# Attention and gated feed-forward on one core: the last third of a unit's gate and value pieces moved into the next unit, ahead of its output products

## The chip, the cores and the metric

The kernel runs on one core of one Trainium2 chip. The time is that of the device for one execution, in microseconds (us), the median of several runs. The profile is one execution of the same program; its span is a little under the run's time (377.5 us of span for a run of 379.3). Engines are called as in the profile: PE is TensorE's matmuls, PEld its weight loads, DVE is VectorE, ACT ScalarE, POOL GpSimd, SP the queue that starts transfers. The granted clock is the share of its full clock at which TensorE was let run.

## The reference

```
# q, k, v: 4 batches x 8 heads x 768 tokens x 64; 16 centroids a head
mask   = cluster(q) == cluster(k)             # a query sees the keys of its own cluster
attn   = softmax(where(mask, q k^T / 8, -1e9)) v
x      = attn, heads side by side             # 3072 tokens x 512
xn     = x / sqrt(mean(x*x) + 1e-6) * rms_g
g, val = xn w_gate, xn w_val                  # 512 -> 1536
out    = (g * sigmoid(g) * val) w_out         # 1536 -> 512
```

## The kernel before

The work is cut into eight units, each half of a batch's queries (384) with all eight heads. In unit u the attention of u is issued step by step (8 heads x 3 steps of two scores matmul blocks), and between the steps a list called `fill` is worked off: the feed-forward layer of the units before. The fill of a unit is spread over the 24 steps by weights.

```python
ps_s = pool("ps_s", 2, space=PSUM)      # scores
ps_a = pool("ps_a", 1, space=PSUM)      # probabilities x values
ps_g = pool("ps_g", 3, space=PSUM)      # everything else, three buffers in rotation
...
def rms(u):                              # RMS step of unit u
    x = xs[u]
    for t in range(HT):
        squares(u, t, True)              # ScalarE
    ...                                  # VectorE: sum, mean, rsqrt (3 Newton steps of 3 operations)
    for t in range(HT):
        nc.vector.tensor_scalar_mul(xn[u][:, t], x[:, t], y[:, t:t + 1])
...
def gv(u, f, val):                       # one piece: four matmuls, a PSUM buffer, a VectorE reader
    ...
    ps = ps_g.tile([P, UQ], F32, tag="gen", name="val" if val else "gate")
    for c in range(CC):
        nc.tensor.matmul(ps, lhsT=w[:, c, f * P:(f + 1) * P], rhs=xnT[u][:, c], ...)
    ...
    if not val:                          # (not the last unit)
        ...
        nc.scalar.activation(th, ps, ACT.Tanh, scale=0.5)
        nc.vector.scalar_tensor_tensor(th, th, 1.0, ps, op0=ALU.add, op1=ALU.mult)
        ...
    else:
        nc.vector.scalar_tensor_tensor(gvT[u][:, f], gates[u], 0.5, ps, op0=ALU.mult, op1=ALU.mult)
...
def out_mm(u, t, part):                  # an output product in three parts of four matmuls
    ...                                  # part 0 takes a buffer of ps_g
    for f in range(4 * part, 4 * part + 4):
        nc.tensor.matmul(outs[u], lhsT=gvT[u][:, f, ...], rhs=wo[:, f], ...)
    if part == 2:
        ...
        nc.vector.tensor_copy(o, outs[u])
        ...
        nc.sync.dma_start(out=..., in_=o)
...
for u in range(NU):
    fill = []
    if u >= 2:
        fill += out_work(u - 2)
    ...
        fill += spread(ffn_work(u - 1), prep)
    ...
    for h in range(H):
        for i in range(3):
            scores(u, h, i)
            if i == 1 and (u, h) != (0, 0):
                pv(u, h - 1) if h else pv(u - 1, H - 1)   # ends with inv and x on VectorE
            if (h, i) == (0, 1) and u:
                rms(u - 1)
            ...
            while n < len(fill) and done <= total * (3 * h + i + 1) / gaps:
                done += fill[n][0]
                fill[n][1]()
                n += 1
    ...
pv(NU - 1, H - 1)
rms(NU - 1)
for _, f in out_work(NU - 2) + ffn_work(NU - 1) + out_work(NU - 1):   # the tail
    f()
```

The traces show VectorE keeping the order of this program. In unit 7 of the kernel before, the first output product was complete at about 304.7 us, and its copy started at 309.81, behind xn, which stands ahead of it.

The softmax here doesn't subtract the row's maximum and nothing guards it: scores larger than these inputs give would overflow.

Of the kernel before, what the change touches and what calls it, by code (L numbers as in the profile page):

```python
# [22 lines left out]
def kernel(  # L23
# [23 lines left out]
    NU = 2 * B  # L47
    CC = DM // P
    FC = DF // P
    scale = 1.0 / (D ** 0.5)  # L50
    KR = D + NC
    WARM = 5
    NQ, NV = 6, 8

    ctx.enter_context(tc.manual_schedule())
# [46 lines left out]
    def busy(n, first=True):  # L102
        to = ps_a.tile([P, 512], F32, tag="acc", name="warm") if first else \
            ps_g.tile([P, 512], F32, tag="gen", name="warm")
        for i in range(n):
            nc.tensor.matmul(to, lhsT=warm[:, :P], rhs=warm, start=True, stop=True)

    busy(WARM)

# [142 lines left out]
    def scores(u, h, i):  # L252
        b, hf = divmod(u, 2)
        g, hh = b * 2 + h // HG, h % HG
        if i == 0:
            pT[u, h] = ptp.tile([P, ST, UQ], BF16, tag="pT", name="pT")
        ps = ps_s.tile([P, 2, 512], F32, tag="s", name="s")
        for j in range(2):
            kc = 2 * i + j
            nc.tensor.matmul(ps[:, j, :UQ], lhsT=kext[g % 4][:KR, hh, kc * P:(kc + 1) * P],  # L260
                             rhs=qext[g % 4][:KR, hh, hf * UQ:(hf + 1) * UQ], start=True, stop=True)
        nc.scalar.activation(pT[u, h][:, 2 * i:2 * i + 2], ps[:, :, :UQ], ACT.Exp, bias=off, scale=scale * ZS)  # L262
# [3 lines left out]
    def pv(u, h):  # L266
        b = u // 2
        g, hh = b * 2 + h // HG, h % HG
        if h == 0:
            xs[u] = xp.tile([P, HT, DM], F32, tag="x", name="x", bufs=2)  # L270
        if h % 2 == 0:
            accs[u] = ps_a.tile([P, 2, HT, D + 1], F32, tag="acc", name="acc")
        acc = accs[u]
        for t in range(HT):
            for kc in range(ST):
                nc.tensor.matmul(acc[:, h % 2, t], lhsT=pT[u, h][:, kc, t * P:(t + 1) * P],  # L276
                                 rhs=vbf[g % 4][:, hh, kc % HT * 2 + kc // HT], start=kc == 0, stop=kc == ST - 1)
        if h % 2:
            inv = small.tile([P, 2, HT], F32, tag="inv", name="inv")
            invs[u] = inv  # L280
            nc.vector.reciprocal(inv, acc[:, :, :, D])
            dst = xs[u][:, :, (h - 1) * D:(h + 1) * D].rearrange("p t (h d) -> p h t d", d=D)
            nc.vector.tensor_tensor(dst, acc[:, :, :, :D], inv.unsqueeze(3).broadcast_to([P, 2, HT, D]), op=ALU.mult)  # L283
# [28 lines left out]
    def xtrans(u, c):  # L312
        if c == 0:
            xnT[u] = xp.tile([P, CC, UQ], BF16, tag="xnT", name="xnT")
        ps = ps_g.tile([P, UQ], BF16, tag="gen", name="tx")
        for t in range(HT):
            nc.tensor.transpose(ps[:, t * P:(t + 1) * P], xn[u][:, t, c * P:(c + 1) * P], ident)  # L317
        nc.vector.tensor_scalar_mul(xnT[u][:, c], ps, gcol[:, c:c + 1])
# [3 lines left out]
    def gv(u, f, val):  # L322
        if f == 0 and not val:
            gvT[u] = xp.tile([P, FC, UQ], BF16, tag="gvT", name="gvT")
        w = wv if val else wg
        ps = ps_g.tile([P, UQ], F32, tag="gen", name="val" if val else "gate")
        for c in range(CC):
            nc.tensor.matmul(ps, lhsT=w[:, c, f * P:(f + 1) * P], rhs=xnT[u][:, c], start=c == 0, stop=c == CC - 1)  # L328
        last = u == NU - 1
        if not val:  # L330
            th = ffn.tile([P, UQ], F32, tag="th", name="th")
            if last:
                nc.scalar.activation(th, ps, ACT.Silu)
                gates[u] = th
# [3 lines that stand above are left out]
                gates[u] = th  # L338
        elif last:
            nc.vector.tensor_mul(gvT[u][:, f], gates[u], ps)  # L340
        else:
            nc.vector.scalar_tensor_tensor(gvT[u][:, f], gates[u], 0.5, ps, op0=ALU.mult, op1=ALU.mult)  # L342
# [3 lines left out]
    def out_mm(u, t, part):  # L346
        b, hf = divmod(u, 2)
        if part == 0:
            outs[u] = ps_g.tile([P, DM], F32, tag="gen", name="o")
        for f in range(4 * part, 4 * part + 4):  # L350
            nc.tensor.matmul(outs[u], lhsT=gvT[u][:, f, t * P:(t + 1) * P], rhs=wo[:, f], start=f == 0, stop=f == FC - 1)  # L351
        if part == 2:
            o = outp.tile([P, DM], F32, tag="o_sb", name="o_sb")
            nc.vector.tensor_copy(o, outs[u])  # L354
            rows = out[b * S:(b + 1) * S].rearrange("(p t) f -> p t f", t=ST)
            nc.sync.dma_start(out=rows[:, 2 * t + hf], in_=o)


    def group_work(g):
        w = []  # L360
        for h in range(HG):
            n = g * HG + h
            w.append((0.25, lambda h=h: trans(g, h, 0)))

            def second(h=h, n=n):
                trans(g, h, 1)
                qcast(g, h)
                kcast(g, h)
                vcast(n)
                load_qk(n + NQ)  # L370
                load_v(n + NV)
            w.append((0.25, second))
        w.append((0.7, lambda: scores_c(g, 0)))
        w.append((0.7, lambda: (scores_c(g, 1), place(nc.gpsimd, nc.gpsimd if g > 1 else nc.sync))))
        return w

    def spread(a, b):

        if not a:
            return list(b)  # L380
        w, n = [], 0
        for i, x in enumerate(a):
            w.append(x)
            while n < len(b) * (i + 1) // len(a):
                w.append(b[n])
                n += 1
        return w

    def ffn_work(u):
        w = [(0.18, lambda c=c: xtrans(u, c)) for c in range(CC)]  # L390
        for f in range(FC):
            w.append((0.64, lambda f=f: gv(u, f, False)))
            w.append((0.64, lambda f=f: gv(u, f, True)))
        return w

    def out_work(u):
        return [(0.86, lambda t=t, p=p: out_mm(u, t, p)) for t in range(HT) for p in range(3)]
# [49 lines left out]
    def second_group():  # L447
        kcast(0, 2, True)
        kcast(0, 3, True)
        for m in range(2):  # L450
            scores_c(1, m)
        for c in range(CC):
            load_gv(c)
        for n in range(HG, H):
            vcast(n)
        place(nc.sync, nc.sync)
        for h in range(HG):
            kcast(1, h)
# [14 lines left out]
    for u in range(NU):  # L473
        fill = []
        if u >= 2:
            fill += out_work(u - 2)
        prep = group_work(u + 2) if 2 <= u < NG - 2 else []
        if u == 0:
            for i in range(2 * H - 6):
                fill += [(0.0 if i else 8.0, lambda: None), (1.0, lambda: busy(1, False))]  # L480
        elif u == 1:
            prep = group_work(2) + group_work(3)
            f0 = ffn_work(0)
            fill = [(0.5, f) for _, f in prep[:8]] + f0[:12] + [(0.0, output_weights)] + spread(f0[12:], prep[8:])
        else:
            fill += spread(ffn_work(u - 1), prep)
        total = sum(c for c, _ in fill)
        gaps, done, n = 3 * H, 0.0, 0
        for h in range(H):
            for i in range(3):  # L490
                scores(u, h, i)
                if (u, h, i) == (0, 0, 1):
                    second_group()
                if i == 1 and (u, h) != (0, 0):
                    pv(u, h - 1) if h else pv(u - 1, H - 1)
                    if (u, h) == (0, 6):
                        second_batch()
                if (h, i) == (0, 1) and u:
                    rms(u - 1)
                if h == H - 1:  # L500
                    squares(u, i, False)
# [4 lines that stand above are left out]
        for _, f in fill[n:]:  # L506
            f()
    pv(NU - 1, H - 1)
    rms(NU - 1)
    for _, f in out_work(NU - 2) + ffn_work(NU - 1) + out_work(NU - 1):  # L510
        f()


# [28 lines left out]
```

## Time and profile before

| | before |
|---|---|
| time | 380.02 us (377.32 to 380.52) |
| span of the profiled run | 377.5 us |
| TensorE busy | 94% of the span |
| ScalarE, VectorE busy | 69%, 63% |
| mean granted TensorE clock | 0.973 |

The page's slices (40 equal ones; each digit the busy share in tenths, PEclk the granted clock in tenths) of the kernel before:

```profile
PE   6979758999989999999999999999999999998995
PEclk9985986999999999999999999999999999999999
```

After slice 9 TensorE is nearly full (eight tenths or more in every slice but the last) and its clock too. What TensorE waited for, the two longest sums (line waited for: us in total, times, longest):

```profile
PE s L260 <- ACT pT L262: 3.6, 5, 2.2
PE tx L317 <- DVE xn L308: 3.2, 2, 2.8
```

No single one of these sums comes to 4 us in 377. The cuts into units and their openings are shown in the prediction.

### The profile page before, as it was taken

The page shows a single profiled execution, that of the slowest core. Times are in us where ns is not written, and L with a number is a line of the kernel's source. Part 1 is how long each engine was busy: PE and PEld are TensorE (multiplying, and loading weights), DVE is VectorE, ACT ScalarE, POOL GpSimd, SP SyncE. Part 2 cuts the span into 40 slices and gives each one's busy share as a digit, 9 for nine tenths or more (in the row PEclk, how much of TensorE's full clock was granted, in tenths as well). Part 3 has the DMA queues.
Part 4 walks back from the last instruction along what each step waited for, and adds up shares of the span by engine and source line. Part 5 has one row for each costly group of instructions (what it writes and reads, how often), then busy time and mean ns, then how long its engine had stood idle before and what let it go on. Part 6 is the DMA issues. An engine that isn't in the chain of part 4 may idle for free.

```text
span 377.5 us, 7991 instructions
## 1 busy us (share of the span) xinstructions
PE 353.5 (94%) x3026; PEld 212.9 (56%) x3026; DVE 238.6 (63%) x573; ACT 261.3 (69%) x461; POOL 107.4 (28%) x221
## 2 busy tenths in 40 slices
PE   6979758999989999999999999999999999998995
PEld 2535445566556655665566655665556656664552
DVE  3882057786766777668766777659756655666432
ACT  4697973789667876788667875888757875882330
POOL 2595062086633135322713134221700000000000
PEclk9985986999999999999999999999999999999999
DMA  7549999726133212232031002000020002001002
GB/s 258 171 105 198 237 334 269 151 60 195 34 121 98 89 43 95 70 125 65 21 128 43 2 9 98 2 0 4 21 84 2 3 5 81 2 0 58 28 3 83
DMA packets 24967, 32.03 MB, mean 85 GB/s; under 512 B 4960, under 2 KB 20832, under 8 KB 24928
## 3 DMA queue, kind: packets, MB, share of 16 engines
q1 hardware_dynamic: 18288, 24.72, 20.0%
q0 software_dynamic: 6064, 6.00, 8.5%
q10 hardware_dynamic: 576, 0.79, 0.6%
q8 instruction: 24, 0.39, 0.4%
q14 instruction: 15, 0.12, 0.1%
HBM read 28.35 MB, written 6.29 MB: 92 GB/s over the span
## 4 chain that ended last, share of the span: by engine, by line
PE 75%; DVE 10%; ACT 6%; DMA 5%; issue 2%; SPq 1%; DVEq 0%; ACTq 0%
PE gate L328 17%; PE val L328 16%; PE s L260 14%; PE o L351 10%; PE acc L276 8%; PE tq L195 5%; PE sc L221 4%; ACT pT L262 3%; DMA qk<-in_q_dram 2%; DMA out_dram<-o_sb 2%; DVE o_sb L354 2%; ACT junk L295 2%; DVE xn L308 1%; PE tx L317 1%; DVE x L283 1%
## 5 line engine op out<-in xcount | busy, mean ns | idle before, releaser
L262 ACT ACTIVATE pT<-s,off 128x768 bf16<-128x768 f32 x192 | 170.9, 901 | 45.0 <-PE s L260 44.5
L260 PE MATMUL s<-qext,kext 80*128 80x384 bf16 x384 | 97.3, 337 | 3.9 <-ACT pT L262 3.6
L328 PE MATMUL gate<-xnT,wg 128*128 128x384 bf16 x384 | 79.2, 327 | 2.1 <-ACT qkT L197 2.1
L328 PE MATMUL val<-xnT,wv 128*128 128x384 bf16 x384 | 78.4, 326 | 0.0
L337 DVE SCALAR_TENSOR_TENSOR th<-th,gate 128x384 f32<-128x384 f32 x84 | 46.4, 552 | 49.3 <-ACT th L336 48.5
L351 PE MATMUL o<-wo,gvT 128*128 128x512 bf16 x288 | 69.3, 379 | 0.0
L201 POOL CAST qext<-qkT 64x384 bf16<-64x384 f32 x64 | 33.4, 522 | 99.8 <-ACT qkT L197 97.9
L260 PEld LDWEIGHTS <-kext 80*128 80x128 bf16 x384 | 37.1, 100 | 38.6 <-issue 14.0
L336 ACT ACTIVATE th<-gate 128x384 f32<-128x384 f32 x84 | 40.9, 487 | 20.4 <-PE gate L328 20.2
L342 DVE SCALAR_TENSOR_TENSOR gvT<-th,val 128x384 bf16<-128x384 f32 x84 | 46.4, 552 | 8.2 <-PE val L328 1.6
L276 PEld LDWEIGHTS <-pT 128*128 128x128 bf16 x1152 | 45.8, 100 | 10.2 <-issue 1.7
L328 PEld LDWEIGHTS <-wg 128*128 128x128 bf16 x384 | 36.4, 97 | 25.4 <-issue 4.0
L328 PEld LDWEIGHTS <-wv 128*128 128x128 bf16 x384 | 36.1, 98 | 23.2 <-issue 2.0
L276 PE MATMUL acc<-vbf,pT 128*128 128x65 bf16 x1152 | 47.7, 196 | 0.5 <-ACT pT L262 0.5
L351 PEld LDWEIGHTS <-gvT 128*128 128x128 bf16 x288 | 27.1, 97 | 27.9
L245 POOL DMA_DIRECT2D qext<-oh x56 | 27.5, 496 | 50.1 <-DVE oh L233 50.0
L197 ACT COPY qkT<-tq 128x384 f32<-128x384 f32 x64 | 29.5, 481 | 13.5 <-PE tq L195 13.0
L195 PE MATMUL tq<-ident_f,qk 128*128 128x128 f32 x192 | 33.3, 294 | 4.4 <-DMA qk<-in_q_dram 3.0
L195 PEld LDWEIGHTS tq<-ident_f,qk 128*128 128x128 f32 x192 | 24.0, 149 | 14.5 <-DMA qk<-in_q_dram 2.6
L209 DVE TENSOR_SCALAR kext<-qkT 64x384 bf16<-64x384 f32 x56 | 21.2, 379 | 9.5 <-ACT qkT L197 8.7
L245 POOL DMA_DIRECT2D kext<-oh x48 | 23.3, 491 | 13.1 <-DVE oh L233 11.4
L354 DVE COPY o_sb<-o 128x512 f32<-128x512 f32 x24 | 15.8, 683 | 16.9 <-DMA out_dram<-o_sb 6.4
(60 smaller groups left out, 232.8 us busy)
## 6 DMA issues: line engine op xcount, KB each, us to landing
qk<-in_q_dram SPq DMA_DIRECT2D x32, 192.0 KB, 3.8
vs<-in_v_dram SPq DMA_DIRECT2D x32, 192.0 KB, 3.7
out_dram<-o_sb SPq DMA_DIRECT2D x24, 256.0 KB, 2.0
qk<-in_k_dram SPq DMA_DIRECT2D x28, 192.0 KB, 3.6
wg<-in_moe_w_gate_dram POOLq DMA_DIRECT2D x4, 384.0 KB, 9.1
wv<-in_moe_w_val_dram POOLq DMA_DIRECT2D x4, 384.0 KB, 10.4
wo<-in_moe_w_out_dram POOLq DMA_DIRECT2D x3, 512.0 KB, 13.4
qext<-oh POOLq DMA_DIRECT2D x56, 12.0 KB, 1.7
```

What stands on the lines that cost most here:

```text
L195: nc.tensor.transpose(ps[:, i * P:(i + 1) * P], qk[:, part, 2 * i:2 * i + 2].rearrange("p t d -> p (t d)"), ident_f)
L197: nc.scalar.copy(qkT[g, h // 2][:, h % 2, part], ps)
L201: nc.gpsimd.tensor_copy(qext[g % 4][:D, h, e * UQ:(e + 1) * UQ], qkT[g, h // 2][e * D:(e + 1) * D, h % 2, 0])
L245: on.dma_start(out=ext[D:D + NC, h, e * UQ:(e + 1) * UQ], in_=oh[32 * h + e * NC:32 * h + (e + 1) * NC])
L260: nc.tensor.matmul(ps[:, j, :UQ], lhsT=kext[g % 4][:KR, hh, kc * P:(kc + 1) * P], rhs=qext[g % 4][:KR, hh, hf * UQ:(hf + 1) * UQ], start=T ...
L262: nc.scalar.activation(pT[u, h][:, 2 * i:2 * i + 2], ps[:, :, :UQ], ACT.Exp, bias=off, scale=scale * ZS)
L276: nc.tensor.matmul(acc[:, h % 2, t], lhsT=pT[u, h][:, kc, t * P:(t + 1) * P], rhs=vbf[g % 4][:, hh, kc % HT * 2 + kc // HT], start=kc == 0 ...
L328: nc.tensor.matmul(ps, lhsT=w[:, c, f * P:(f + 1) * P], rhs=xnT[u][:, c], start=c == 0, stop=c == CC - 1)
L336: nc.scalar.activation(th, ps, ACT.Tanh, scale=0.5)
L337: nc.vector.scalar_tensor_tensor(th, th, 1.0, ps, op0=ALU.add, op1=ALU.mult)
L342: nc.vector.scalar_tensor_tensor(gvT[u][:, f], gates[u], 0.5, ps, op0=ALU.mult, op1=ALU.mult)
L351: nc.tensor.matmul(outs[u], lhsT=gvT[u][:, f, t * P:(t + 1) * P], rhs=wo[:, f], start=f == 0, stop=f == FC - 1)
```

## The change

The intent can be guessed from the diff: a part of the feed-forward work that is left over from one unit comes first in the next, so that the fill of unit 1 is lighter and there is TensorE work ahead of the output products.

```diff
+    CUT = CC + 2 * FC - 8
...
         if u >= 2:
-            fill += out_work(u - 2)
+            fill += ffn_work(u - 2)[CUT:] + out_work(u - 2)
...
-            f0 = ffn_work(0)
+            f0 = ffn_work(0)[:CUT]
...
-            fill += spread(ffn_work(u - 1), prep)
+            fill += spread(ffn_work(u - 1)[:CUT], prep)
...
-    for _, f in out_work(NU - 2) + ffn_work(NU - 1) + out_work(NU - 1):
+    for _, f in ffn_work(NU - 2)[CUT:] + out_work(NU - 2) + ffn_work(NU - 1) + out_work(NU - 1):
```

`ffn_work` has 4 transposes and 24 gate and value pieces; `CUT` leaves the last 8 pieces (f = 8 to 11) out. The RMS step keeps its place, in the second step of a unit, and ahead of everything in the tail.

## The prediction

> **What bounds the kernel now.** I cut the run into its units first. The chain of work that ended last shows a block of eight output-product matmuls (line L351) at 94.74, 137.37, 179.49, 221.54, 263.66 and 301.22 us; each opens a unit of the loop, so units 2 to 7 begin just before these times, unit 1 fills 50 to 94.7, and the tail after the loop 338.1 to 377.5. The busy time of each engine in these stretches (columns: stretch, its length, then busy us of PE, PEld, DVE, ACT, POOL, then the granted clock, DMA share, GB/s):
>
> ```profile
> 50.00:94.70 44.70, 39.63 (x366) 25.11 (x364) 32.85 (x76) 32.44 (x59) 20.64 (x40) 0.92 0.73 197
> 137.30:179.40 42.10, 41.39 (x378) 25.58 (x377) 29.46 (x72) 31.58 (x57) 13.74 (x28) 1.00 0.26 81
> ...
> 301.20:338.10 36.90, 36.24 (x335) 22.31 (x333) 21.93 (x55) 27.62 (x49) 0.00 (x0) 1.00 0.06 22
> 338.10:377.50 39.40, 33.50 (x200) 17.72 (x198) 17.18 (x42) 9.67 (x22) 0.00 (x0) 1.00 0.11 41
> ```
>
> TensorE idles about 0.7 us in a unit of 42.1, and the clock is full. Busy matmul time can flatter, so I checked it by pace. One gate or value piece (four matmuls) takes 0.65 us in the chain, an output piece 0.86, a pair of scores matmuls 0.33, a block of 18 probability-value matmuls 0.55 (timeline, start to the next start). For unit 7: 24 x 0.65 + 9 x 0.86 + 24 x 0.33 + 8 x 0.55 = 35.7, plus 12 transposes of about 0.06, is 36.4 of 36.9 us. So in units 2 to 7 TensorE sets the time, without slack: whatever stops it for a microsecond costs a microsecond. Second, I read what the other engines do at the opening of a unit, for there the change works. Unit 7, in order of time:
>
> ```profile
> 301.06 1.89 PE L351 MATMUL o<-wo,gvT 128*128 128x512 bf16 x8
> ...
> 303.12 0.71 PE L276 MATMUL acc<-vbf,pT 128*128 128x65 bf16 x18
> ...
> 304.10 0.56 DVE L283 TENSOR_TENSOR x<-acc,inv 128x384 f32<-128x384 f32 x1
> ...
> 306.05 0.16 DVE L302 TENSOR_TENSOR sm<-ss 128x3 f32<-128x3 f32 x1 [1.40 <-ACT junk L295]
> ...
> 308.62 1.28 DVE L308 TENSOR_SCALAR xn<-x,ny 128x512 bf16<-128x512 f32 x3
> ...
> 309.81 1.28 DVE L354 COPY o_sb<-o 128x512 f32<-128x512 f32 x2
> ```
>
> The last head of the former unit arrives (acc), VectorE scales it (x), waits 1.40 us for ScalarE's squares, runs a chain of small operations, and writes xn: from 304.66 to 309.90, VectorE serves nobody else. The first output product was complete by about 304.7, yet its copy comes after xn at 309.81: VectorE keeps program order. TensorE does not feel it, because three output products of 2.6 us each have three PSUM buffers (ps_g, three slots in rotation) and need no reader until the third is done.
>
> [...]
>
> ```profile
> 57.09 0.29 PE L317 MATMUL tx<-ident,xn 128*128 128x128 bf16 x1 [2.82 <-DVE xn L308]
> ```
>
> (the timeline of TensorE), and in the busy times by microsecond, whose first column after the engines is the clock:
>
> ```profile
> 57.00:58.00 1.00, 0.55 (x2) 0.21 (x2) 1.00 (x4) 0.00 (x0) 1.00 (x2) 0.50 1.06 381
> ...
> 62.00:63.00 1.00, 1.00 (x5) 0.47 (x4) 0.00 (x0) 0.24 (x1) 0.00 (x0) 0.50 1.12 209
> 63.00:64.00 1.00, 1.00 (x6) 0.49 (x4) 0.55 (x1) 0.85 (x2) 0.00 (x0) 0.69 1.14 245
> ```
>
> A wait of 2.82 us for xn in unit 1 is followed by clock 0.50 from about 56.8 to 63.6[...]. A wait of 2.20 us at 22.8 us has 0.50 from 26.1 to 36.3[...]; two of 0.51 and 0.99 us close together before 46.5 have it from 46.6 to 50.0[...]; one of 1.50 us in the tail has none. [...] the trace has just three table loads, and the last (1283 ns, for Silu in the tail) has time to spare, so I count nothing for tables.
>
> **The change, part by part.** No operation is added or removed. Of the 24 gate and value pieces of a unit, 8 (f = 8 to 11) move into the next unit, before its output pieces.
>
> Unit 1 loses 8 x 0.65 = 5.2 us of TensorE work, units 2 to 7 lose 8 and gain 8, the tail gains 8. The fill per step of unit 1 falls from 24.88/24 = 1.04 to 19.76/24 = 0.82 weight units, so its wait for xn shrinks by perhaps 0.9 us (one pair of scores and one block of 18 come ahead of it), but the second half has denser transposes, with short waits for ScalarE's copies. I choose -5.2 for unit 1.
>
> Opening of units 2 to 7. A gate or value piece needs a PSUM buffer like an output product, but a new one every piece, and it is freed by VectorE operations (552 ns each, lines L337 and L342) that stand in VectorE's queue by program order. By the weights 0.64 and the loop's rule, two pieces (gate 8, value 8) are issued before the RMS chain; gate 9 and value 9 directly behind it; then gate 10, value 10. With time 0 at the unit's first scores pair: gate 8 and value 8 end at 1.63, scores at 1.96, the block of 18 at 2.5. ScalarE's queue (the former unit's Exp and a Square, as at 300.5 to 302.7 now) lets Tanh 8 finish at about 2.4, VectorE's two operations on it end at 3.6, and only then x follows: 4.4, against 3.9 now (304.66 less the unit's first scores pair, 300.73). From x to xn's end is 5.24 us as read above: 9.65. The reader of gate 9 is next: 10.2. TensorE meanwhile writes gate 9, value 9 (its buffer was gate 8's) and gate 10 (value 8's), and comes to value 10 at 4.8 to 5.1; its buffer is gate 9's. It stops until 10.2, so for 5.1 to 5.4 us, say 5.2. From the idle 0.6 to 0.7 us of now I take back 0.3, the waits of the transposes at the end of the output products, since the copies now come in time. Net 4.9 x 6 = 29.4 us. After the stop VectorE is one piece ahead again and no second stop follows.
>
> Tail. Now TensorE runs output products for 7.8 us under the chain, then waits 1.50 us:
>
> ```profile
> 347.14 0.50 PE L317 MATMUL tx<-ident,xn 128*128 128x128 bf16 x6
> 348.40 0.69 DVE L354 COPY o_sb<-o 128x512 f32<-128x512 f32 x1 [1.59 <-DMA out_dram<-o_sb]
> 349.14 0.65 PE L317 MATMUL tx<-ident,xn 128*128 128x128 bf16 x6 [1.50 <-DVE o_sb L354]
> ```
>
> After it, all eight pieces come behind the chain: gate 8, value 8 and gate 9 fill the buffers from 339.4 to 341.35, value 9 waits for the reader of gate 8, which follows xn's end at 345.6 and takes 0.55: a stop of 4.85 us. The five pieces left are paced by VectorE at up to 1.1 us a pair and end at about 349.3, so the output products begin 9.9 us later than now; the transposes behind them save about 0.8 of the 1.50. Net 9.1.
>
> Clock. [...] I put the end of the drop 3.3 to 6.7 us after work resumes, mean 5; at half clock this loses 2.5 us, a little less where TensorE has gaps: 2.3 x 7 = 16 us. This is an estimate from the three drops' lengths in this trace.
>
> Sum: 380.0 - 5.2 + 29.4 + 9.1 + 16 = 429; rounded down for stops that run partly under the drop: 427.
>
> **The rivals.** Work is only rearranged: TensorE is full, unit 1 loses 5.2, the tail gains 5.2 less 0.8, and each unit saves its 0.3: about 377, or within 2%. For it speaks that counts and bytes are equal, and that pieces in the tail would cover the RMS chain; against it that these pieces need VectorE, which the output products did not. Second rival: the stop comes but the clock holds: 413. Against it are drops after 2.20 and 2.82 us; for it, none after 1.50. Third: the lost time is ScalarE's, because Exp, Tanh and squares crowd at the opening; but ScalarE is busy 31.6 of 42.1 us and the same pieces leave the unit's end, so it would cost under 1 us a unit: 382.
>
> **Range and chances.** Without drops 413[...]. I take 411 to 438. The order of VectorE's queue and the three buffers are read, not guessed, so slower by over 2% gets 0.92, within 2% 0.05, faster 0.03.
>
> **What would show it.** Right: in each of units 2 to 7 a TensorE wait of about 5 us at a value piece, released by L337 of VectorE, directly behind xn; units of about 47 us, or 49 with clock 0.50 after the stop; a stop near 5 us in the tail; unit 1 some 5 us shorter; output copies no longer held by xn. Wrong: no such wait (more buffers in effect, or another order on VectorE), stops of under 2 us, or clock 1.00 throughout units 2 to 7.

No term of the sum is cut: 380.0 - 5.2 + 29.4 + 9.1 + 16 = 429, rounded down to 427. The 16 us for the clock is the author's estimate. It has a drop at each of the seven stops, since waits of 2.20 and 2.82 us had been followed by one and the stops are longer; the 3.3 to 6.7 us until the clock comes back are estimated from the lengths of that trace's three lows, 10.2, 3.4 and 6.8 us (26.1 to 36.3, 46.6 to 50.0, 56.8 to 63.6), and what sets the end of a low was not shown. The upper end of the range, 438, was the estimate for lows as long as the longest of these at every stop.

## The result, and the profile after

The changed kernel takes 428.5 us (427.37 to 429.53, four runs) against 378.67 of the kernel before (four runs), ratio 1.132 with a 95% interval of 1.124 to 1.139. Ratios here are the mean time of one kernel's fast runs over that of the other's of the same rounds, so not quite the ratio of the medians. It is correct, and slower by about 50 us. Forecast were 427.

The slices of the changed kernel:

```profile
PE   7979669976999499995999779995999689959996
PEclk9968989996999979996999969998899979998999
```

Where the kernel before has an almost unbroken row of nines, there is now a hole every four to five slices (a slice is 10.6 us, a unit 44 to 51), and the clock dips with it. TensorE's longest waits:

```profile
PE val L329 <- DVE th L338: 37.5, 8, 5.4
PE s L261 <- ACT pT L263: 3.9, 6, 2.2
```

The first line is new: value pieces wait for VectorE's operation on the gate (lines have moved by one: L329 is the old L328). The same cut into units (columns as in the prediction: stretch, length, busy us of PE, PEld, DVE, ACT, POOL, clock, DMA share, GB/s), for unit 1, unit 3, unit 7 and the tail:

```profile
44.12:87.56 43.44, 35.87 (x349) 22.39 (x348) 29.12 (x69) 33.50 (x63) 19.65 (x37) 0.96 0.74 195
...
138.07:188.06 49.99, 44.37 (x381) 26.70 (x377) 30.27 (x71) 32.35 (x57) 13.68 (x29) 0.93 0.22 68
...
331.61:376.20 44.59, 38.99 (x341) 23.64 (x339) 23.00 (x56) 28.73 (x49) 0.00 (x0) 0.92 0.05 19
376.20:425.60 49.40, 39.91 (x226) 21.16 (x226) 21.19 (x50) 10.97 (x26) 0.00 (x0) 0.95 0.09 33
```

Unit 3 has the same number of VectorE and ScalarE instructions, within one, as before, but takes 49.99 us instead of 42.1, at a clock of 0.93; TensorE's busy time grew too, from 41.4 to 44.4 us, for the same matmuls. The opening of unit 6 in order of time:

```profile
291.11 0.56 DVE L284 TENSOR_TENSOR x<-acc,inv 128x384 f32<-128x384 f32 x1
...
291.34 0.81 PE L329 MATMUL gate<-xnT,wg 128*128 128x384 bf16 x4
...
293.06 0.16 DVE L303 TENSOR_TENSOR sm<-ss 128x3 f32<-128x3 f32 x1 [1.40 <-ACT junk L296]
...
295.77 1.31 DVE L309 TENSOR_SCALAR xn<-x,ny 128x512 bf16<-128x512 f32 x3
...
297.00 0.53 DVE L338 SCALAR_TENSOR_TENSOR th<-th,gate 128x384 f32<-128x384 f32 x1
297.58 1.44 PE L329 MATMUL val<-xnT,wv 128*128 128x384 bf16 x4 [5.11 <-DVE th L338]
```

The gate piece at 291.34 (gate 10) is the last that finds a PSUM buffer. Its follower, value 10, wants the buffer of gate 9, whose reader is the th at 297.00, directly behind xn. TensorE waits 5.11 us, then needs 1.44 us for four matmuls that took 0.81: the clock stands at 0.50. The clock is the column after the five engines:

```profile
293.00:294.00 1.00, 0.00 (x0) 0.00 (x0) 0.81 (x4) 1.00 (x3) 1.00 (x4) 1.00 0.13 33
294.00:295.00 1.00, 0.00 (x0) 0.00 (x0) 0.82 (x6) 1.00 (x3) 1.00 (x3) 0.76 0.11 25
...
298.00:299.00 1.00, 1.00 (x5) 0.46 (x4) 0.66 (x2) 0.00 (x0) 0.00 (x0) 0.50 0.00 0
...
301.00:302.00 1.00, 1.00 (x20) 0.86 (x19) 0.42 (x1) 0.88 (x1) 0.00 (x0) 0.83 0.00 0
```

It falls to 0.50 within the stop, at 294.5, and returns to 1.00 at 301.35, 3.8 us after the work did. The tail has the same stop, and the old wait at the transposes behind the output products shrinks from 1.50 to 0.45 us:

```profile
381.99 1.28 DVE L309 TENSOR_SCALAR xn<-x,ny 128x512 bf16<-128x512 f32 x3
383.18 0.55 DVE L338 SCALAR_TENSOR_TENSOR th<-th,gate 128x384 f32<-128x384 f32 x1
383.78 1.44 PE L329 MATMUL val<-xnT,wv 128*128 128x384 bf16 x4 [4.63 <-DVE th L338]
...
397.16 0.65 PE L318 MATMUL tx<-ident,xn 128*128 128x128 bf16 x6 [0.45 <-DVE o_sb L355]
```

Where the 48.0 us between the two profiled spans come from, by the starts of the units' first scores matmul (the tail from the start of the last block of 18; by this cut unit 1 of the kernel before begins at 45.06, not at 50):

| part | forecast | measured |
|---|---|---|
| up to unit 1 | 0 | -0.9 |
| unit 1 | -5.2 | -5.7 |
| units 2 to 7 | 29.4 and 13.8 for the clock | 7.9, 7.9, 6.8, 7.9, 7.1, 6.8: together 44.3 |
| tail | 9.1 and 2.3 for the clock | 10.4 |

### The profile page after: what moved, and what is told of

Same layout as the page of the kernel before. It is cut to its first block, busy times and chain, and to the rows that moved or that the text cites. A ratio compares the mean times of both kernels' runs of the same rounds, so it can differ in the third digit from the quotient of the medians.

```text
span 425.6 us, 7990 instructions
## 1 busy us (share of the span) xinstructions
PE 366.6 (86%) x3026; PEld 216.4 (51%) x3026; DVE 243.0 (57%) x573; ACT 264.2 (62%) x461; POOL 107.7 (25%) x221
## 4 chain that ended last, share of the span: by engine, by line
PE 62%; DVE 24%; ACT 9%; issue 3%; DMA 2%; SPq 0%; DVEq 0%; ACTq 0%
PE o L352 15%; PE val L329 12%; PE gate L329 11%; PE s L261 11%; PE acc L277 7%; PE tq L196 4%; ACT pT L263 4%; ACT junk L296 3%; DVE th L338 3%; DVE xn L309 3%; DVE gvT L343 3%; DVE ohT L231 2%; DVE oh L234 2%; DVE mx L229 2%; DVE scT L225 1%
## 5 line engine op out<-in xcount | busy, mean ns | idle before, releaser
L329 PE MATMUL val<-xnT,wv 128*128 128x384 bf16 x384 | 84.9, 347 | 37.8 <-DVE th L338 37.5
L261 PE MATMUL s<-qext,kext 80*128 80x384 bf16 x384 | 99.5, 344 | 4.0 <-ACT pT L263 3.9
L329 PE MATMUL gate<-xnT,wg 128*128 128x384 bf16 x384 | 83.9, 342 | 2.0 <-DVE xnT L319 1.4
L329 PEld LDWEIGHTS <-wv 128*128 128x128 bf16 x384 | 38.6, 102 | 67.6 <-issue 46.9
L343 DVE SCALAR_TENSOR_TENSOR gvT<-th,val 128x384 bf16<-128x384 f32 x84 | 46.5, 554 | 12.9 <-PE val L329 5.9
L277 PEld LDWEIGHTS <-pT 128*128 128x128 bf16 x1152 | 46.6, 101 | 10.6 <-issue 2.4
L329 PEld LDWEIGHTS <-wg 128*128 128x128 bf16 x384 | 37.7, 101 | 25.6 <-issue 7.9
L198 ACT COPY qkT<-tq 128x384 f32<-128x384 f32 x64 | 29.4, 482 | 6.1 <-PE tq L196 5.5
L210 DVE TENSOR_SCALAR kext<-qkT 64x384 bf16<-64x384 f32 x56 | 22.3, 398 | 14.8 <-ACT qkT L198 13.7
L196 PEld LDWEIGHTS tq<-ident_f,qk 128*128 128x128 f32 x192 | 22.6, 146 | 14.3 <-DMA qk<-in_q_dram 3.1
L296 ACT ACTIVATE junk<-x 128x384 bf16<-128x384 f32 (+1 forms) x48 | 20.1, 419 | 14.1 <-DVE x L284 13.6
## 6 DMA issues: line engine op xcount, KB each, us to landing
wv<-in_moe_w_val_dram POOLq DMA_DIRECT2D x4, 384.0 KB, 10.4
```

Of the source, the lines that this page charges most:

```text
L196: nc.tensor.transpose(ps[:, i * P:(i + 1) * P], qk[:, part, 2 * i:2 * i + 2].rearrange("p t d -> p (t d)"), ident_f)
L198: nc.scalar.copy(qkT[g, h // 2][:, h % 2, part], ps)
L261: nc.tensor.matmul(ps[:, j, :UQ], lhsT=kext[g % 4][:KR, hh, kc * P:(kc + 1) * P], rhs=qext[g % 4][:KR, hh, hf * UQ:(hf + 1) * UQ], start=T ...
L277: nc.tensor.matmul(acc[:, h % 2, t], lhsT=pT[u, h][:, kc, t * P:(t + 1) * P], rhs=vbf[g % 4][:, hh, kc % HT * 2 + kc // HT], start=kc == 0 ...
L296: nc.scalar.activation(junk[:, c], xs[u][:, t, c], ACT.Square, accum_out=sq[u][:, int(last), t:t + 1])
```

## The experiments

The theory: VectorE works in program order, the readers of the moved pieces stand behind the RMS chain, TensorE stops until they come, and the stop drops its clock. Rivals were ScalarE's crowding, the number of PSUM buffers, a cost in proportion to the pieces moved, and VectorE's backlog as the cause of the slow time after a stop. All kernels start from the changed one; all gave correct results. Each was timed beside the kernel before on its own chip; the changed kernel itself was not run again, so a difference to its 428.5 us is one between chips. The kernel before differs by under 1 us between them (378.67 to 379.44).

**e1: the RMS step behind the moved pieces.**

```diff
-            fill += ffn_work(u - 2)[CUT:] + out_work(u - 2)
+            fill += ffn_work(u - 2)[CUT:] + [(0.0, lambda u=u: rms(u - 1))] + out_work(u - 2)
...
-                if (h, i) == (0, 1) and u:
+                if (h, i) == (0, 1) and u == 1:
                     rms(u - 1)
... (the tail)
+    for _, f in ffn_work(NU - 2)[CUT:]:
+        f()
     rms(NU - 1)
-    for _, f in ffn_work(NU - 2)[CUT:] + out_work(NU - 2) + ffn_work(NU - 1) + out_work(NU - 1):
+    for _, f in out_work(NU - 2) + ffn_work(NU - 1) + out_work(NU - 1):
```

> The changed kernel, but the RMS step of the former unit is issued behind the eight moved pieces and ahead of the output products (in units 2 to 7 and in the tail). Theory (VectorE's program order: the readers of the pieces stand behind the RMS chain): all TensorE waits at value pieces of about 5 us vanish, clock 1.00 through units 2 to 7, time 376 us (372 to 379), so at or a little under the kernel before. Rival (the pieces cost because Exp, Tanh and VectorE work crowd at the unit's opening wherever the RMS step stands): over 400 us, waits at value pieces stay.

Measured: 378.84 us, ratio to before 0.998 (0.994 to 1.002). The whole loss is gone with the eight pieces still moved. The opening of unit 6 in its timeline:

```profile
267.90 0.81 PE L329 MATMUL val<-xnT,wv 128*128 128x384 bf16 x4
...
268.88 1.03 PE L352 MATMUL o<-wo,gvT 128*128 128x512 bf16 x3
...
271.17 0.16 DVE L303 TENSOR_TENSOR sm<-ss 128x3 f32<-128x3 f32 x1 [1.86 <-ACT junk L296]
...
273.74 1.28 DVE L309 TENSOR_SCALAR xn<-x,ny 128x512 bf16<-128x512 f32 x3
```

The chain (sm to xn) now runs under the output products, as in the kernel before. Units 3 to 5 take 41.7 us. The version gains nothing either: in its profile unit 1 is 3.3 us shorter than in the kernel before (45.92 for 49.18) and the tail 4.2 us longer (43.59 for 39.37), so what is moved out of unit 1 comes back in the tail. One wait at a value piece is left, 1.52 us in unit 2, and the median is 3 us above the 376 expected, inside the stated range; in the profiled run, the slowest of the six, unit 1 had the clock at 0.50 for 10.2 us (57.9 to 68.1) where the kernel before had 6.8 (56.8 to 63.6); the mean clocks are 0.968 and 0.973.

**e2: only VectorE's part of the RMS step behind the pieces.** ScalarE's squares stay where they were.

```diff
-    def rms(u):
-        x = xs[u]
+    def rms_squares(u):
         for t in range(HT):
             squares(u, t, True)
+
+    def rms(u):
+        x = xs[u]
 # loop and tail as e1, and rms_squares where rms was:
                 if (h, i) == (0, 1) and u:
-                    rms(u - 1)
+                    rms_squares(u - 1)
+                    if u == 1:
+                        rms(u - 1)
```

> As e1, but ScalarE's squares stay in their old place (ahead of Tanh 9) and only VectorE's part of the RMS step is issued behind the moved pieces. Theory: most of the stop goes, but ScalarE still waits for x and does three squares before Tanh 9, so the reader of gate 9 ends at about 7.0 us instead of 10.2: a stop of about 2.2 us is left in units 2 to 7 and 1.5 in the tail; 389 us without clock drops, up to 400 with them, say 391. Rival 1 (ScalarE's order is the whole cause): 428 as the changed kernel. Rival 2 (VectorE's chain is the whole cause, ScalarE none): 376.

Measured: 393.04 us, ratio 1.036 (1.030 to 1.042). The seven stops are still there but last 1.25 to 1.90 us; the opening of unit 6:

```profile
273.08 0.47 ACT L339 ACTIVATE th<-gate 128x384 f32<-128x384 f32 x1
...
273.59 0.56 DVE L340 SCALAR_TENSOR_TENSOR th<-th,gate 128x384 f32<-128x384 f32 x1 [1.77 <-ACT th L339]
274.19 0.81 PE L331 MATMUL val<-xnT,wv 128*128 128x384 bf16 x4 [1.57 <-DVE th L340]
```

Now VectorE waits 1.77 us for ScalarE's Tanh, which stands behind the squares. So about a third of a stop (11.8 us of 36.0 over the seven) is there from ScalarE's order alone; in the changed kernel it lies beside the longer VectorE chain. Both of the extreme rivals (428 and 376) fall. Only one of the seven stops is followed by a lower clock; the mean clock of the profiled run is 0.965, against 0.930 in the changed kernel.

**e3: dummy matmuls in the stop.** They write to the attention's buffer, which is free there.

```diff
-            fill += ffn_work(u - 2)[CUT:] + out_work(u - 2)
+            m = ffn_work(u - 2)[CUT:]
+            fill += m[:5] + [(0.0, lambda: busy(20))] + m[5:] + out_work(u - 2)
 # tail: m[:3] + busy(19) + m[3:]
```

> The changed kernel with 20 dummy matmuls of 512 columns (0.216 us each, 4.3 us; 19 in the tail) issued just where TensorE stops, into another PSUM buffer, so that TensorE is busy during the stop. The stop itself stays. Theory (the stop has two costs, the wait and the halved clock after it): clock 1.00 through units 2 to 7, time 428.5 - 15 = 413.5 us (410 to 417); 15 is half of the 30 us in which the changed kernel's TensorE worked at clock 0.50 after its stops. Rival (the time after the stop is lost to VectorE's backlog and not to the clock): 428 or more.

The 0.216 us expected for a dummy is the pace of the output products in the kernel before, where 36 matmuls of 512 columns took 7.76 us (339.38 to 347.14).

Measured: 414.58 us, ratio 1.093 (1.088 to 1.097), 14 us under the changed kernel with more work in it. Unit 6, from TensorE's timeline and from the busy times of the units:

```profile
285.30 4.48 PE L107 MATMUL warm<-warm 128*128 128x512 bf16 x19
290.57 0.81 PE L329 MATMUL val<-xnT,wv 128*128 128x384 bf16 x4 [0.79 <-DVE th L338]
```

```profile
279.96:322.80 42.84, 41.12 (x358) 24.53 (x357) 24.38 (x59) 27.87 (x49) 7.43 (x16) 1.00 0.08 25
```

The value piece still starts where VectorE lets it (a record of one of the twenty dummies is missing from the trace), but its four matmuls take 0.81 us instead of 1.44, and the clock is 1.00 in the unit. VectorE's backlog is the same here (behind the th that frees the value piece its next two operations start 0.63 and 1.11 us later, as in the changed kernel), so it is not what made the time after a stop slow.

**e4 and e7: two pieces moved instead of eight**, the RMS step behind them in the tail only. In a unit, both fall into the first step, so their readers come before the RMS chain, as unit 6 of e4 shows:

```profile
264.21 0.52 DVE L338 SCALAR_TENSOR_TENSOR th<-th,gate 128x384 f32<-128x384 f32 x1
264.82 0.56 DVE L343 SCALAR_TENSOR_TENSOR gvT<-th,val 128x384 bf16<-128x384 f32 x1
...
267.48 0.16 DVE L303 TENSOR_TENSOR sm<-ss 128x3 f32<-128x3 f32 x1 [1.40 <-ACT junk L296]
```

```diff
-    CUT = CC + 2 * FC - 8
+    CUT = CC + 2 * FC - 2
 # tail as e1
```

> Only two pieces (gate 11, value 11) are moved, and in the tail the RMS step follows them. Both are issued in the first step of a unit, so their readers stand ahead of the RMS chain in VectorE's queue. Theory: no stop in units 2 to 7, 377 us (374 to 380). Rival (each moved piece costs its share): a quarter of 50, so 391 us.

> The kernel of e4 again, in more rounds, to see whether it beats the kernel before. From e4 (units of 41.58 us against 42.12, ratio 0.994): 377.3 us, ratio 0.990 to 0.997. If e4 was chance: ratio 1.000 within 0.003.

Measured: 377.33 us, ratio 0.994 (0.989 to 0.998) and, in five rounds, 376.41 us, ratio 0.993 (0.990 to 0.996). Moving two pieces costs nothing as such; unit 3 of e4:

```profile
137.04:178.62 41.58, 41.35 (x379) 25.65 (x377) 29.83 (x72) 31.70 (x57) 13.68 (x29) 1.00 0.27 82
```

That is 0.5 us shorter than the kernel before at the same busy time. The short waits of the kernel before at the transposes and first gate pieces behind the output products (0.45 to 0.76 us a unit) are not in e4's trace. This is the one version that beats both kernels, by 0.7%: its interval leaves 1 out.

**e5: four pieces moved.**

```diff
-    CUT = CC + 2 * FC - 8
+    CUT = CC + 2 * FC - 4
 # tail as e1
```

> Four pieces (f = 10, 11) are moved, and in the tail the RMS step follows them. Two have their readers ahead of the RMS chain, two behind it. With four pieces the three PSUM buffers do not run out before the first output product. Theory (order on VectorE is the cause, buffers only say where TensorE notices it): TensorE stops all the same, but at an output product's third part, which reads the gvT of f = 11, about 4.6 us in units 2 to 5 and 3.7 in units 6 and 7, with clock drops: 413 us (405 to 420). Rival 1 (three PSUM buffers are the cause): no stop, 377 us. Rival 2 (dose): half of 50, 403 us, with stops at value pieces.

Measured: 414.06 us, ratio 1.091 (1.084 to 1.097). TensorE stops in units 2 to 7, 20.9 us in all, at an output product (waits at value pieces stay under 0.5 us); unit 5:

```profile
247.59 1.31 DVE L309 TENSOR_SCALAR xn<-x,ny 128x512 bf16<-128x512 f32 x3
248.82 0.53 DVE L338 SCALAR_TENSOR_TENSOR th<-th,gate 128x384 f32<-128x384 f32 x1
249.81 0.55 DVE L343 SCALAR_TENSOR_TENSOR gvT<-th,val 128x384 bf16<-128x384 f32 x1 [0.46 <-DVE th L338]
...
250.41 0.61 PE L352 MATMUL o<-wo,gvT 128*128 128x512 bf16 x1 [4.39 <-DVE gvT L343]
```

The output product reads gvT, whose maker stands behind xn. No buffer is short here, and the stop is nearly as long (3.9 to 4.4 us in units 2 to 5, expected 4.6; about 2.2 in units 6 and 7, expected 3.7). So running out of PSUM buffers is not needed for the stop; here it decides where TensorE meets the late reader. No run had more than three buffers. The dose rival falls too: four pieces cost 35 us, more than half of 50, and two cost nothing.

**e6: a longer chain.**

```diff
-        for i in range(3):
+        for i in range(6):      # Newton steps of rsqrt, three operations each
```

> The changed kernel with six instead of three Newton steps in the RMS chain: nine more small VectorE operations of about 0.197 us each from start to start, 1.77 us a chain. Theory: each of the seven stops grows by 1.77 us, 12.4 us in all, clock drops perhaps a little shorter or longer: 441 us (438 to 445). Rival (the stop is set by ScalarE or by a transfer, not by VectorE's chain): under 432 us.

The 0.197 us is the pace of the chain in the changed kernel: nine such operations start from 96.20 to 97.78 us, 0.197 us apart.

Measured: 443.48 us, ratio 1.168 (1.162 to 1.174). TensorE's wait at value pieces grows from 37.5 to

```profile
PE val L329 <- DVE th L338: 49.8, 8, 7.2
```

that is by 12.3 us, against 12.4 expected. The time grows by 15.0 (443.48 - 428.5); in four of the stops the clock now stays low for 10.24 us instead of 6.83, and in the tail for 6.83 instead of 3.41; the mean clock is 0.910 against 0.930. Work resumed 33.9 us in all before the clock did, against 30.0 in the changed kernel; half of that difference, 2 us, is most of the rest.

**e8: two pieces, with the tail of the changed kernel** (RMS step ahead of them).

```diff
-    CUT = CC + 2 * FC - 8
+    CUT = CC + 2 * FC - 2
```

> As e4, but the tail has the RMS step ahead of the two pieces, as the changed kernel has. Theory: no stop in units 2 to 7, one in the tail, at an output product's third part that needs the gvT of f = 11, whose makers stand behind the RMS chain: about 4.3 us, of which 3.5 reach the end, and perhaps 1.5 for the clock: 382 us (380 to 384). Rival (a stop needs the PSUM buffers to run out, and two pieces and three output products do not do that early): 377, as e4.

Measured: 381.34 us, ratio 1.006 (1.002 to 1.009), 5 us above e7 of the same rounds. The tail:

```profile
340.36 1.28 DVE L309 TENSOR_SCALAR xn<-x,ny 128x512 bf16<-128x512 f32 x3
341.56 0.55 DVE L338 SCALAR_TENSOR_TENSOR th<-th,gate 128x384 f32<-128x384 f32 x1
342.21 0.56 DVE L343 SCALAR_TENSOR_TENSOR gvT<-th,val 128x384 bf16<-128x384 f32 x1
342.82 7.26 PE L352 MATMUL o<-wo,gvT 128*128 128x512 bf16 x25 [3.58 <-DVE gvT L343]
```

Even two pieces make a stop (3.58 us, 4.3 expected) as soon as their readers are issued behind the chain.

## Why the prediction was right

*TensorE sets the time in units 2 to 7, without slack.* Right: the forecast stops took 31.4 us, the stop at value 9 of unit 2 took 1.5, and the low clock after the stops half of 27.1; that is 46.5, and the units grew by 44.3. The 2.2 us between are 0.37 a unit, where the forecast took back 0.3 for the waits of the transposes. In e1 and e4, with no stop there, units 3 to 5 take 41.6 to 41.7 us.

*The stop of 5.2 us in each of units 2 to 7.* Right in size, place and releaser: 5.30, 5.44, 5.30, 5.44, 5.11 and 4.82 us, mean 5.24, always at value 10 and always released by the th of gate 9. That its length is that of the chain is shown by e6, and that program order is its cause by e1. In unit 3 the stop ends 10.6 us after the unit's first scores pair, where 10.2 was forecast. The forecast put its end on VectorE alone; e2 shows that ScalarE's squares, ahead of Tanh 9, would hold up to 1.9 us by themselves.

*The three PSUM buffers.* The place was right, but as a cause this was half the story: e5 stops without running out of them. The prediction did not see that the output product behind the pieces needs their gvT in any case.

*No second stop.* Right behind the chain; but unit 2 has another one, of 1.52 us, earlier, at value 9. It was not forecast. It is also in e1, e2, e3 and e6, where eight pieces are moved, and not in e4 and e5, with two and four. In the trace VectorE is at work on the cluster masks of unit 1's end (scT to oh, L225 to L234) from 87.39 us on, and the th of gate 8 comes directly behind them, at 92.13; that they are the cause is read from this order, no run takes it apart.

*The clock.* Right in kind: a drop at each of the seven stops. By the trace's record of the clock, the work in units 2 to 7 resumed 3.58, 5.90, 3.83, 6.01, 3.77, 4.02 and, in the tail, 2.90 us before the clock did, 30.0 in all, mean 4.3 where 5 was forecast. Half of 30 is 15 us, forecast 16; e3 gets back 14. The forecast's lengths came from only three drops, of which one (from 56.8 us) began before its wait was over at 57.09: that the mean came out this near is in part luck. Which waits bring a drop, these runs do not settle. In the kernel before, waits of 2.20 and 2.82 us did, with TensorE busy for 1.21 and 0.88 us of the 3.41 us (the shortest low of that trace) ahead of the drops at 26.08 and 56.80; so did one of e2's seven stops of 1.25 to 1.90 us. With 1.91 us busy of 3.41 there was a drop at 46.56, after waits of 0.51 and 0.99 us, and none at 350.35, around the single 1.50 us of the tail; nor did 0.51 and 1.03 us bring one in the changed kernel. The lows of these two kernels after a wait lasted 3.41, 6.83 or 10.24 us.

*Unit 1 and the tail.* -5.7 for -5.2, and 10.4 for 11.4. The first is luck in part: in the five profiles with eight pieces moved unit 1 takes 43.4 (the changed kernel), 44.8, 44.9, 45.9 and 45.9 us, against 49.2 before, and the clock stood at 0.50 for 10.2 us of it before and for 3.4 after, which the forecast left out. In the tail the drop lasted 3.41 us only (383.27 to 386.68). The wait at the transposes shrank by 1.05 us, forecast 0.8.

The parts before rounding add up to a growth of 49.3 us; the medians differ by 49.8 and the profiled spans by 48.0. It came this near because the small errors have both signs.

## What to carry to other kernels

When work is moved ahead of something, look at who reads its result and what stands ahead of that reader on the reader's engine: work whose reader is held by a long chain covered here only as much of it as the free buffers held: three pieces, then a stop of 5.11 us (unit 6). Output products could cover the RMS chain because three of them needed no reader for 7.8 us; gate and value pieces could not. If such pieces are to come first, issue the chain behind their readers (e1, e4), and count a stop of several microseconds on TensorE with a part for the clock, here 2 us on each 5 (14 us over seven stops, e3).
